# A fused transformer backward on one core: the ds tile copied as fp32 pairs, and the sums of dx through ScalarE and GpSimd

## The chip, the core and the metric

The program runs on one core of a Trainium2 chip. The metric is the device time of one execution in microseconds (us), as the median of several runs; lower is better. Engines are named as in the profile: PE (TensorE matmul), PEld (TensorE weight load), DVE (VectorE), ACT (ScalarE), POOL (GpSimd) and SP (SyncE, which issues DMAs). "L924" is line 924 of the kernel before.

## What is computed

The reference takes x (2048 tokens, 448 features), layer-normalises it, and adds to x a 16-head attention block (head size 28) and a SwiGLU block with 1792 hidden units. The kernel returns the output and, for a given gradient of it, the gradients of x and of the five weight matrices:

```python
def _fwd_reference(A_x, A_wqkv, A_wo, B_x, B_w_gate, B_w_up, B_w_down):
    x = A_x
    xn = _layernorm(x, axis=-1)
    return x + _A_ref(xn, A_wqkv, A_wo) + _B_ref(xn, B_w_gate, B_w_up, B_w_down)
...
_out, _vjp = jax.vjp(_f, A_x, A_wqkv, A_wo, B_w_gate, B_w_up, B_w_down)
```

Two pieces matter here. For each pair of heads and each block of 128 queries by 512 keys, the attention backward needs ds = exp(scores) * dp, and then the gradient of the queries, which takes ds transposed. The gradient of x is a sum over tokens of many matrix products: the gate and up paths of SwiGLU, and the gradients of q, k and v times the transposed projection weights.

## The kernel before, in words

The program is written in a fixed order per engine: what the Python code emits first on an engine runs first on it. Waits are only by data and by buffers. Up to about 617 us the forward pass and the weight gradients of SwiGLU run. What the change touches lies behind that, in the attention backward, and ends with it at about 1397 us; a tail to 1438 us finishes dx.

The attention backward is a loop over 512 steps (4 head groups, 2 head pairs, 4 key chunks, 4 query chunks, 4 query blocks of 128). Here four successive steps are called a **quad**; there are 128. On each step:

- `row` (L826) has PE compute two score tiles "sb" (L834) and, for the step before, two dp tiles "db" (L842), each 128x512 fp32 in one PSUM bank. There are three sb and three db buffers.
- `ew` (L854) has ACT take the exponential of the sb tiles into bf16 "e_sb" (L858), and DVE multiply db by e_sb into bf16 "ds_sb" (L864). Reading sb and db is what frees them.
- For the first three steps of a quad a DMA transposes ds_sb into "dsT" (L851). For the last step PE transposes it in `tr_unit` (L914): eight 128x128 bf16 transposes (L919) into one db buffer, seen there as 128x1024 bf16, and one ACT copy to dsT (L924). In the last quad alone a second one is copied by DVE (L922).
- `kv` (L926) accumulates the k and v gradients in the single PSUM tile "acc" (L937, L941). At the end of a key chunk, once in four quads, ACT copies acc out (L947, "dkv").
- `dq_unit` (L958), once per quad, multiplies dsT of the quad before into the PSUM tile "genb" (L968), and ACT copies it out: into dq_acc for the first key chunk (L972), else into dq_st (L981), which POOL then adds (L983, L985). On the last head group's last key chunk DVE does it (L977).

Between these the program places **fillers**: one unit of other work per quad, split over the four places of the step, whose products accumulate in genb, of which there is one buffer. So dq and filler units alternate in it. The unit ends behind `tr_unit` at the start of a quad, with its last matmuls and one operation that takes genb out. In order the fillers are: the last SwiGLU weight columns (`late_dw`, L898, to 662 us), y units (`y_unit`, 7 or 11 matmuls, out by DVE, L1098 and L1101, 675 to 890 us), and the units of dx that the change touches:

- `dx_unit` (L1137): 48 units, in three passes fq over the hidden units. Pass 0 has 10 matmuls a unit (L1149) and ends with an ACT copy into the fp32 SBUF sum "dxg" (L1155); it runs from 924 to 1024 us. Passes 1 (8 matmuls) and 2 (10 matmuls) end with a DVE add of genb to dxg (L1157), from 1029 to 1263 us.
- `dc_unit` (L1189): 16 units of 8 matmuls (L1196), which end with a DVE add (L1200), from 1293 to 1388 us.

Units for the q, k and v weight gradients stand between them (`dsp_unit`, `dsq_unit`, `dwq_unit`).

The order on PE around the end of a quad is: row, two filler matmuls, the eight transposes, the unit's last matmuls, row, two or three kv steps, dq, row, kv, filler matmul, row, four filler matmuls, row. On ACT the copy of L924 stands ahead of the copy of L1155, and both ahead of the next row's two exponentials.

The tail (`dx_mm`, `dx_a`, `dx_b`) reads dxg, on DVE for 13 of the 16 token blocks (L1315), and POOL adds the final terms (L1332).

Of the kernel before, what the change touches and what calls it, by code (L numbers as in the profile page):

```python
# [9 lines left out]
ALU = mybir.AluOpType  # L10
AX = mybir.AxisListType
FP32 = mybir.dt.float32
# [5 lines left out]
D = 448  # L18
# [7 lines left out]
P = 128  # L26
# [79 lines left out]
def kernel(  # L106
# [23 lines left out]
    PE, DVE, ACTE, POOL, SP = nc.tensor, nc.vector, nc.scalar, nc.gpsimd, nc.sync  # L130
# [539 lines left out]
    for t in range(4):  # L670
        run(T_unit(xnT, xn_t, t, t % 2 == 0, ps_s if t < 2 else None))
    DVE.tensor_reduce(out=r_ones[:],
                      in_=ident_f[:].rearrange("p (a b) -> p a b", b=HP)[:, :, 28:30],
# [11 lines left out]
    for c in range(3):  # L685
        k = 4 * c
        t = 4 * c + 4
# [106 lines left out]
    def have(*keys):  # L794
        for x in [x for x in slow if x[1] in keys]:
            slow.remove(x)
            SP.dma_start(out=x[2], in_=x[3])
# [23 lines left out]
    def flush(upto):  # L821
        while held and held[0][0] <= upto:
            _, o, i = held.pop(0)
            (POOL if now < NB else SP).dma_start(out=o, in_=i)
# [89 lines left out]
    def tr_unit(b):  # L914
        for qi in (3,) if b < NB // 4 - 1 else (2, 3):
            ds = dss.pop(4 * b + qi)
            ps = ps_b.tile([P, 8, P], BF16, name="db", bufs=3)
            for c in range(8):
                PE.transpose(ps[:, c, :], ds[:, c // 4, (c % 4) * P:(c % 4 + 1) * P], ident_bf[:])  # L919
            o = dsT[b][:, qi].rearrange("p j kt s -> p (j kt) s")  # L920
            if qi == 2:
                DVE.tensor_copy(out=o, in_=ps[:])  # L922
            else:
                ACTE.copy(out=o, in_=ps[:])  # L924

    def kv(k):  # L926
        g, hp, kc, qc, qi = steps[k]
# [30 lines left out]
    def dq_unit(b):  # L958
# [27 lines left out]
        if qc == 3:  # L986
            for j in range(2):
                dst = dqkvc_d[crow(g, 0, 2 * hp + j), :].rearrange("r (a q s) -> r a q s", q=2, s=P)
                for par in range(2):
                    r = 64 * par + HP * j  # L990
                    store(dst[:, :, par], dqT[g][r:r + DH, hp].rearrange("r (a s) -> r a s", s=P))
            if hp == 1:
                stream[3:3] = [(480, lambda hp=hp: dsq_unit(g, hp)) for hp in range(2)]
                at = [i for i, u in enumerate(stream) if u[1] in (dx_open, tail_open)]
                at = max(at[0] + 1, 5) if at and g != 1 else 5
                s_done.add((g, "w"))
                stream[at:at] = [(2270, lambda c=c: dwq_unit(g, c)) for c in range(4)]
# [108 lines left out]
    dxs = {}  # L1106
    dxgst = ExitStack()
# [4 lines left out]
    def dx_open():  # L1112
        flush(10 ** 9)
        yst.close()
        gp = dxgst.enter_context(tc.tile_pool(name="dxgp", bufs=1, reuse_waits="tile"))
        dxs["g"] = gp.tile([P, NT, D], FP32, name="dxg")
        st = dxst.enter_context(tc.tile_pool(name="dxp", bufs=2, reuse_waits="tile"))
        dxs["pool"] = st
        load_w(0, now + 15)
        load_dx(0, 0)  # L1120
        return
        yield

    def load_w(fq, due):
        f0, f1 = FQ[fq]
        w = dxs["w", fq] = dxs["pool"].tile([P, 5, 2, D], BF16, name="wguT")
        drip(("dx", 0, fq), [(w[:, i - f0:min(i + 2, f1) - f0], wT_d[:, i:min(i + 2, f1), :, :D]) for i in range(f0, f1, 2)], due)

    def load_dx(ch, fq):
        f0, f1 = FQ[fq]  # L1130
        if ch == 2 and fq < 2:
            load_w(fq + 1, now + 32)
        d = dxs["pool"].tile([P, 5, 2, 512], BF16, name="dau_c")
        drip(("dx", ch, fq), [(d[:, i - f0:min(i + 2, f1) - f0], F_d[ch, :, i:min(i + 2, f1), 1:3, :]) for i in range(f0, f1, 2)], now + 16)
        dxs[ch, fq] = d

    def dx_unit(ch, fq, ti):  # L1137
        if ti == 0:
            have(("dx", ch, fq))
            nxt = 4 * fq + ch + 1  # L1140
            if nxt < 12:
                load_dx(nxt % 4, nxt // 4)
        d = dxs[ch, fq]
        f0, f1 = FQ[fq]
        n = 2 * (f1 - f0)
        tsl = slice(ti * P, (ti + 1) * P)
        ps = ps_g.tile([P, 512], FP32, name="genb")
        for i in range(n):
            PE.matmul(ps[:, :D], lhsT=d[:, i // 2, i % 2, tsl], rhs=dxs["w", fq][:, i // 2, i % 2, :],  # L1149
                      start=(i == 0), stop=(i == n - 1))  # L1150
            if i < n - 1:
                yield 189
        o = dxs["g"][:, 4 * ch + ti, :]
        if fq == 0:
            ACTE.copy(out=o, in_=ps[:, :D])  # L1155
        else:
            DVE.tensor_tensor(out=o, in0=ps[:, :D], in1=o, op=ALU.add)  # L1157
        yield 189


# [23 lines left out]
    def load_dc(ch):  # L1184
        dcs[ch] = dxs["tw"].tile([P, NCP, 512], BF16, name="dc")
        src = dqkvc_d[:, ch * 512:(ch + 1) * 512].rearrange("(i p) s -> p i s", p=CP)
        drip(("dc", ch), [(dcs[ch][:CP, a:b], src[:, a:b]) for a, b in ((0, 3), (3, 6), (6, 8))], now + 16)

    def dc_unit(t):  # L1189
        if t % 4 == 0:  # L1190
            have(("dc", t // 4))
            if t < 12:
                load_dc(t // 4 + 1)
        ps = ps_g.tile([P, 512], FP32, name="genb")
        for i in range(NCP):
            PE.matmul(ps[:, :D], lhsT=dcs[t // 4][:CP, i, (t % 4) * P:(t % 4 + 1) * P], rhs=dxs["wq"][:CP, i, :],  # L1196
                      start=(i == 0), stop=(i == NCP - 1))
            if i < NCP - 1:
                yield 189
        DVE.tensor_tensor(out=dxs["g"][:, t, :], in0=ps[:, :D], in1=dxs["g"][:, t, :], op=ALU.add)  # L1200
        yield 189

    def push(*units):
# [2 lines left out]
    for ch in range(4):  # L1206
        for half in range(2):
            for ti in range(4):
                stream.append((189 * (7 + 4 * half), lambda a=(ch, half, ti): y_unit(*a)))
    stream.append((0, dx_open))  # L1210
    for fq in range(3):
        for ch in range(4):
            for ti in range(4):
                stream.append((189 * 2 * (FQ[fq][1] - FQ[fq][0]), lambda a=(ch, fq, ti): dx_unit(*a)))
    stream.append((0, tail_open))
    for t in range(NT):
        stream.append((189 * NCP, lambda t=t: dc_unit(t)))
# [119 lines left out]
    for k in range(NB + 12):  # L1337
        now = k
        if k < NB:
            g, hp, kc, qc, qi = steps[k]  # L1340
# [18 lines left out]
        if m == 0:  # L1359
            b = (k - 8) // 4  # L1360
            if 9 <= k < NB and cur is None:
                fill_open(600)
            fill_step(R0)
            if 0 <= b < NB // 4:
                tr_unit(b)
            fill_step(BIG)
        elif m == 1:
            b = (k - 13) // 4
            if 0 <= b < NB // 4:
                dq_unit(b)  # L1370
            if k > NB and k < NB + 8:
                while stream:
                    for _ in stream.pop(0)[1]():
                        pass
                if k < NB + 4:
                    dx_mm(0)
                else:
                    dx_a(0)
                    dx_mm(2)
        elif m == 2:  # L1380
            if 9 <= k < NB:
                fill_open(BIG)
                fill_step(R2)
        else:
            fill_step(R3)
# [59 lines left out]
```

## Time and profile before

| | |
|---|---|
| time, median of 3 runs | 1437.01 us |
| the three runs | 1435.54, 1437.01, 1440.87 us |
| span of the profiled execution, first to last instruction | 1438.2 us |
| attention backward, first to last exponential | about 617 to 1391 us |
| ds_sb multiplies on DVE (L864) | 1024 of 685 ns mean |
| exponentials on ACT (L858) | 1024 of 611 ns mean |
| copies of the transposed ds on ACT (L924), 128x1024 bf16 | 128 of 1016 ns mean |
| copies into dxg on ACT (L1155), 128x448 fp32 | 16 of 560 ns mean |
| adds into dxg on DVE (L1157, L1200), 128x448 fp32 | 32 of 620 ns and 16 of 616 ns mean |
| POOL adds of 128x256 fp32 (L983) and 128x512 fp32 (L396) | 724 and 1274 ns mean |

The profiled execution's own time is known as its span; it lies amid the three times and is 1.2 us above their median. A line of the timeline view holds the start, the length, the engine, the line, the operation with what it writes and reads, and how many instructions of the kind were merged; an engine starts an instruction before the one ahead has fully ended, so lengths overlap, and the distance of two starts is what an instruction takes from its engine. A line of the stage table has the stretch, its length, and then for each engine named in the header the busy time and the number of instructions, and at the end PE's granted clock, the DMA share and GB/s.

### The profile page before, as it was taken

The numbers are of one execution on the slowest core, as the hardware profiler recorded it, in microseconds if no ns is written. First come the engines' busy times: TensorE is split into PE (matmuls) and PEld (weight loads), VectorE is DVE, ScalarE is ACT, GpSimd is POOL, SyncE is SP. The second block draws the span as 40 slices with busy tenths as digits, with TensorE's granted clock in tenths as the row PEclk, the third lists the DMA queues.
The fourth block names the chain that finished last, engine by engine and source line by source line (L and its number), as shares of the span: only waits on it lengthen the run. The fifth ranks groups of instructions, "written<-read, shape, count | busy, mean of one in ns | idle before, by whom it ended". The sixth has DMA issues, their size and how long they took to land. (4 is left out here: it accounts for less than half of the span.)

```text
span 1438.2 us, 34638 instructions
## 1 busy us (share of the span) xinstructions
PE 1321.2 (92%) x12625; PEld 539.0 (37%) x12686; DVE 1154.8 (80%) x2001; ACT 1264.2 (88%) x2190; POOL 411.8 (29%) x577
## 2 busy tenths in 40 slices
PE   5899999989999999989999989999999999999995
PEld 2333333333333333333343434433443334443333
DVE  6677757656666676578999989888899999999988
ACT  4799988989889998869999989999989999899974
POOL 6574514454434454211121211201111112020005
PEclk9999999999999999989999999999999999999998
DMA  5796957796578676699999999999999999999981
GB/s 154 183 205 160 237 116 169 179 190 157 149 164 191 153 155 153 176 243 233 219 213 227 206 227 173 221 219 223 223 169 200 200 216 218 212 186 207 190 142 60
DMA packets 681116, 270.22 MB, mean 188 GB/s; under 512 B 607338, under 2 KB 655970, under 8 KB 680946
## 3 DMA queue, kind: packets, MB, share of 16 engines
q1 hardware_dynamic: 672498, 254.78, 87.1%
q0 software_dynamic: 7040, 12.93, 4.1%
q8 instruction: 99, 1.62, 0.5%
q14 instruction: 71, 0.58, 0.1%
q10 hardware_dynamic: 1408, 0.30, 0.1%
HBM read 64.37 MB, written 59.62 MB: 86 GB/s over the span
## 5 line engine op out<-in xcount | busy, mean ns | idle before, releaser
L864 DVE TENSOR_TENSOR ds_sb<-db,e_sb 128x512 bf16<-128x512 f32 x1024 | 646.5, 685 | 48.6 <-issue 22.4
L858 ACT ACTIVATE e_sb<-sb 128x512 bf16<-128x512 f32 x1024 | 555.0, 611 | 53.7 <-PE db L842 37.1
L628 ACT ACTIVATE eT<-s_w 128x1024 bf16<-128x1024 f32 x256 | 263.8, 1030 | 47.0 <-PE s_ps L625 43.8
L630 ACT ACTIVATE eT<-s_ps 128x512 bf16<-128x512 f32 x512 | 280.2, 611 | 0.0
L842 PE MATMUL db<-kd,qd 32*128 32x512 bf16 x1024 | 238.0, 385 | 8.6 <-DVE ds_sb L864 7.5
L834 PE MATMUL sb<-kd,qd 32*128 32x512 bf16 x1024 | 210.9, 389 | 5.3 <-DMA qd<-QD_d 3.4
L983 POOL TENSOR_TENSOR dq_acc<-dq_acc,dq_st 128x256 f32<-128x256 f32 x64 | 46.4, 724 | 497.7 <-ACT dq_st L981 497.7
L941 PE MATMUL acc<-ds_sb,qd 128*32 128x512 bf16 x1024 | 161.3, 391 | 0.0
L937 PE MATMUL acc<-e_sb,qd 128*32 128x512 bf16 x1024 | 159.2, 392 | 1.3 <-DVE dw_o L544 1.3
L924 ACT COPY dsT<-db 128x1024 bf16<-128x1024 bf16 x128 | 130.0, 1016 | 18.4 <-PE db L919 17.3
L396 POOL TENSOR_TENSOR nn<-nn,ag 128x512 f32<-128x512 f32 x56 | 71.3, 1274 | 249.7 <-DVE ag L394 241.1
L625 PE MATMUL s_ps<-QQ,KK 32*128 32x512 bf16 x512 | 126.2, 385 | 4.1
L1149 PE MATMUL genb<-wguT,dau_c 128*128 128x448 bf16 x448 | 117.5, 355 | 6.3 <-ACT dq_st L981 3.9
L625 PE MATMUL s_w<-QQ,KK 32*128 32x512 bf16 x512 | 100.2, 387 | 12.8 <-ACT eT L628 9.8
L834 PEld LDWEIGHTS <-qd 32*128 32x128 bf16 x1024 | 48.2, 91 | 146.3 <-issue 136.9
L437 PE MATMUL gen<-xn_t,f_sp 128*128 128x448 bf16 x416 | 91.8, 354 | 2.6 <-DVE nn L411 1.7
L437 PEld LDWEIGHTS <-f_sp 128*128 128x128 bf16 x640 | 55.7, 98 | 76.7 <-issue 31.6
L919 PE MATMUL db<-ident_bf,ds_sb 128*128 128x128 bf16 x1032 | 80.3, 222 | 0.9 <-DVE ds_sb L864 0.9
L968 PE MATMUL genb<-dsT,kd 128*32 128x256 bf16 x2048 | 79.2, 274 | 1.1
L919 PEld LDWEIGHTS <-ds_sb 128*128 128x128 bf16 x1032 | 69.1, 99 | 23.6 <-issue 5.1
L397 POOL TENSOR_TENSOR nn<-nn,tt 128x512 f32<-128x512 f32 x56 | 72.1, 1287 | 4.4
L625 PEld LDWEIGHTS <-KK 32*128 32x128 bf16 x1024 | 29.1, 91 | 115.3 <-issue 112.5
(179 smaller groups left out, 1951.7 us busy)
## 6 DMA issues: line engine op xcount, KB each, us to landing
F_d<-hda SPq DMA_DIRECT2D x56, 384.0 KB
dau_c<-F_d SPq DMA_DIRECT2D x24, 512.0 KB
qd<-QD_d SPq DMA_DIRECT2D x16, 512.0 KB
kd<-KD_d SPq DMA_DIRECT2D x16, 384.0 KB
dsT<-ds_sb SPq DMA_TRANSPOSE x383
h_c<-F_d SPq DMA_DIRECT2D x8, 512.0 KB
wT_d<-wT_f SPq DMA_DIRECT2D x14, 256.0 KB
KD_d<-qk_sp SPq DMA_DIRECT2D x7, 512.0 KB
```

The costliest lines, as they stand in the source:

```text
L437: PE.matmul(ps[:, :D], lhsT=fsp[fc][:, t // 4, w, t % 4, :], rhs=rhs[:, t, :], start=(t == 0), stop=(t == NT - 1))
L625: PE.matmul(sp4[hh], lhsT=KK[g][r:r + HP, kt * P:(kt + 1) * P], rhs=QQ[g][r:r + HP, qsl], start=True, stop=True, tile_position=(r, 0))
L628: ACTE.activation(out=e2[0][:], in_=wide[:], func=ACT.Exp, scale=SCALE)
L630: ACTE.activation(out=e2[1][:, j], in_=sp4[2 + j], func=ACT.Exp, scale=SCALE)
L834: PE.matmul(s_ps[:], lhsT=qside[g, qc][r:r + HP, 0, qi * P:(qi + 1) * P], rhs=kside[g, kc][r:r + HP, 0, :], start=True, stop=True, tile_po ...
L842: PE.matmul(d_ps[:], lhsT=qside[g, qc][r:r + HP, 1, qi * P:(qi + 1) * P], rhs=kside[g, kc][r:r + HP, 1, :], start=True, stop=True, tile_po ...
L858: ACTE.activation(out=est[k][:, j], in_=sps.pop((k, j))[:], func=ACT.Exp, scale=SCALE)
L864: DVE.tensor_tensor(out=ds[:, j], in0=dps.pop((k - 1, j))[:], in1=est[k - 1][:, j], op=ALU.mult)
L919: PE.transpose(ps[:, c, :], ds[:, c // 4, (c % 4) * P:(c % 4 + 1) * P], ident_bf[:])
L924: ACTE.copy(out=o, in_=ps[:])
L937: PE.matmul(a[r:r + HP, :], lhsT=sp4[:, 1, r:r + HP], rhs=e[:, j, :], start=first, stop=last, tile_position=(0, r), skip_group_check=True)
L941: PE.matmul(a[r:r + HP, :], lhsT=sp4[:, 0, r:r + HP], rhs=ds[:, j, :], start=first, stop=last, tile_position=(0, r), skip_group_check=True)
```

## The change

The copy of the transposed ds by ACT reads and writes its 128x1024 bf16 as 128x512 fp32, the same bytes. The copy by DVE for the last quad stays. The 48 adds into dxg leave DVE: ACT copies genb to an fp32 staging tile "gst" (two buffers), and POOL adds that to dxg. Pass 0 still copies directly. No instruction of PE or SP is added or moved.

```diff
             if qi == 2:
                 DVE.tensor_copy(out=o, in_=ps[:])
             else:
-                ACTE.copy(out=o, in_=ps[:])
+                ACTE.copy(out=o.bitcast(FP32), in_=ps[:].bitcast(FP32))
...
         dxs["g"] = gp.tile([P, NT, D], FP32, name="dxg")
+        dxs["st"] = dxgst.enter_context(tc.tile_pool(name="gsp", bufs=2, reuse_waits="tile"))
...
+    def add_in(o, ps, first):
+        if first:
+            ACTE.copy(out=o, in_=ps[:, :D])
+            return
+        st = dxs["st"].tile([P, D], FP32, name="gst")
+        ACTE.copy(out=st[:], in_=ps[:, :D])
+        POOL.tensor_tensor(out=o, in0=o, in1=st[:], op=ALU.add)
...
-        o = dxs["g"][:, 4 * ch + ti, :]
-        if fq == 0:
-            ACTE.copy(out=o, in_=ps[:, :D])
-        else:
-            DVE.tensor_tensor(out=o, in0=ps[:, :D], in1=o, op=ALU.add)
+        add_in(dxs["g"][:, 4 * ch + ti, :], ps, fq == 0)
...
-        DVE.tensor_tensor(out=dxs["g"][:, t, :], in0=ps[:, :D], in1=dxs["g"][:, t, :], op=ALU.add)
+        add_in(dxs["g"][:, t, :], ps, False)
```

## The prediction

> **What bounds the kernel now.** I read the page's busy shares first, then the table of stages over the attention backward, then the timelines of single quads.
>
> ```profile
> PE 1321.2 (92%) x12625; PEld 539.0 (37%) x12686; DVE 1154.8 (80%) x2001; ACT 1264.2 (88%) x2190; POOL 411.8 (29%) x577
> ```
>
> Three engines look nearly full, so the shares decide nothing. By stages (busy us of PE, PEld, DVE, ACT, POOL):
>
> ```profile
> core 0: us, PE busy (x) PEld busy (x) DVE busy (x) ACT busy (x) POOL busy (x), PEclk, DMA share, GB/s
> 924.10:1009.50 85.40, 81.68 (x926) 33.63 (x925) 70.87 (x113) 81.54 (x159) 9.80 (x14) 1.00 1.13 222
> 1029.00:1160.40 131.40, 126.07 (x1461) 52.75 (x1458) 123.27 (x214) 121.72 (x227) 17.91 (x28) 1.00 1.06 196
> 1160.40:1262.50 102.10, 97.66 (x1135) 41.92 (x1134) 96.04 (x156) 93.62 (x175) 13.97 (x21) 0.98 1.15 214
> ```
>
> The first row is pass 0, where ACT copies into dxg: ACT is busy 95%, DVE 83%. The others are passes 1 and 2, where DVE adds: DVE 94%, ACT 93 and 92%. So pass 0 is ACT's, and in the others it is open whether DVE's add is on the path. The timelines tell. Pass 0, ACT and then PE:
>
> ```profile
> 948.53 1.02 ACT L924 COPY dsT<-db 128x1024 bf16<-128x1024 bf16 x1
> 949.42 0.56 ACT L1155 COPY dxg<-genb 128x448 f32<-128x448 f32 x1
> 949.85 1.13 ACT L858 ACTIVATE e_sb<-sb 128x512 bf16<-128x512 f32 x2
> ...
> 954.44 1.02 ACT L924 COPY dsT<-db 128x1024 bf16<-128x1024 bf16 x1
> 955.33 0.56 ACT L1155 COPY dxg<-genb 128x448 f32<-128x448 f32 x1
> ```
> ```profile
> 954.21 0.73 PE L1149 MATMUL genb<-wguT,dau_c 128*128 128x448 bf16 x3
> ...
> 955.46 0.38 PE L937 MATMUL acc<-e_sb,qd 128*32 128x512 bf16 x2
> ...
> 955.94 0.62 PE L968 MATMUL genb<-dsT,kd 128*32 128x256 bf16 x16
> ```
>
> A quad takes 954.44-948.53 = 5.91 us. The unit's product is complete at 954.94 (954.21+0.73), but ACT is in L924 and takes genb out only from 955.33 to 955.89. The dq products (L968) need genb and start at 955.94. PE's last kv pair starts 955.46 and occupies 0.22 (kv pairs follow each other at 0.22), so PE stood idle about 0.25.
>
> Pass 1, DVE and then PE:
>
> ```profile
> 1125.66 0.62 DVE L1157 TENSOR_TENSOR dxg<-genb,dxg 128x448 f32<-128x448 f32 x1
> 1126.19 1.28 DVE L864 TENSOR_TENSOR ds_sb<-db,e_sb 128x512 bf16<-128x512 f32 x2
> 1127.63 3.74 DVE L864 TENSOR_TENSOR ds_sb<-db,e_sb 128x512 bf16<-128x512 f32 x6 [0.16 <-ACT dq_acc L972]
> 1131.29 0.62 DVE L1157 TENSOR_TENSOR dxg<-genb,dxg 128x448 f32<-128x448 f32 x1
> ```
> ```profile
> 1130.26 0.61 PE L919 MATMUL db<-ident_bf,ds_sb 128*128 128x128 bf16 x8
> ...
> 1130.99 0.39 PE L834 MATMUL sb<-kd,qd 32*128 32x512 bf16 x2
> 1131.00 0.80 PE L842 MATMUL db<-kd,qd 32*128 32x512 bf16 x2
> 1131.72 0.39 PE L937 MATMUL acc<-e_sb,qd 128*32 128x512 bf16 x2
> ```
>
> The quad takes 1131.29-1125.66 = 5.63. The two db products of the row at 1131.00 took 0.80 where a pair takes 0.39: the second waits for its buffer, which the last of the six multiplies frees at 1131.37 (1127.63+3.74). So the ring is: six multiplies on DVE, second db, kv and dq on PE, next row, its db, first of the next six multiplies. **The add lies outside it.** DVE does the add and two multiplies while PE goes through kv and dq, and DVE is idle before the next six (the 0.16 above), waiting for the row. A quad with 7-matmul y units has the same 5.63 (timeline, L924 at 747.50 and 753.13), and the quad from 675.05 to 680.74, with no DVE add in it, took 5.69. Pass 2, with two more matmuls, takes 5.69 (L924 at 1171.79 and 1177.48); y units with 11 take 5.85 (L924 at 771.07 and 776.92): there PE sets the pace.
>
> Once in four quads ACT copies acc out as well (L947, 0.72). There ACT is the path: pass 1 takes 6.31 (L924 at 1130.93 and 1137.24), pass 0 6.75 (935.87 and 942.62).
>
> **The change, part by part.** The built program has the same PE and SP orders; ACT gains 48 copies, DVE loses 48 adds, POOL gains 48 adds.
>
> *The pair copy.* No row shows it. Bounds: 1.016 us if it goes by bytes, as now; 0.56 (L1155, 448 fp32 to fp32) as the nearest smaller row. Per element: L924's 1024 in 1.016 and L858's 512 in 0.61 differ by 0.8 ns an element, L858 and L1155 by 0.8 as well, though L1155 moves 1792 bytes a partition in 0.56 and L924 2048 in 1.016. So elements count, and I take 0.61. Start to start L924 takes 0.89, an exponential 0.49: 0.40 less for ACT, 128 times, 51 us of ACT's 1264. It pays only where ACT is the path:
>
> - Pass 0, 12 plain quads: the copy to dxg starts when the product is complete, 954.99 instead of 955.33, and dq no longer waits: 0.25 each, 3.0 us. Next late is the ring above and PE, as in pass 2 (5.69), which 5.91-0.25 = 5.66 meets.
> - Pass 0, 4 quads with the acc copy: ACT is the path through copy, exponentials, L947 and dq's copy, and all start 0.33 earlier (again bound by the product): 1.3 us.
> - Quads with the acc copy in the y units and late_dw, where ACT is the path (645, 692, 741, 788, 862): L947 moves up until acc is complete. At 741: acc complete at 742.81, L947 now at 743.05, new 742.87: 0.18 each, 0.9 us.
> - Elsewhere nothing: L924 is done long before dsT is read a quad later, and its db buffer is wanted only by the second row behind it (1127.08, free at 1126.32).
>
> *The db buffers.* The built program hands the three db buffers out in another order in the first quads. In quads 1, 6, 7, 8 (633, 663, 669, 675) the row behind the transposes has the transposes' own buffer for its second db, so it waits for ACT's copy instead of DVE. At 669: copy 669.16+0.61 plus 0.06 is 669.83, now 669.71: 0.12 later, three times; at 633 about 0.4. A loss of 0.8 us. From quad 9 the order is as before.
>
> *ACT for DVE in passes 1 and 2 and dc.* DVE loses 48 x 0.54 (start to start at 1125.66) = 26 us. In plain quads of pass 1 and dc the ring does not hold it: 0. In pass 2 the two multiplies behind the add start 0.10 sooner, which spares PE a short wait for ds: 0.04 each, 12 quads, 0.5 us. With L977 on DVE and at the last unit some 0.3 us. ACT: pair copy 0.49 and new copy 0.43 are 0.92 where L924 took 0.89: 0.03 later exponentials, hidden in plain quads by ACT's own wait (0.20 before the L858 at 1129.96). Cover gone, they cost that 0.03 a quad, 1.4 us. In the 13 quads with the acc copy ACT is the path: 9 at 0.05, and 4 of pass 2, where the product is complete 0.1 later, at 0.12: a loss of 0.9 us. Behind the new copy on ACT stand the exponentials, and dq on PE waits for genb: 1125.79 to 1126.35, wanted at 1126.54.
>
> *POOL.* A 448 add lies between 0.724 (256) and 1.274 (512): about 1.14 by the line through both. A unit comes each 5.7 us and POOL is busy 0.7 of them; staging has two buffers: hidden, and dxg is read first at 1397.54, the last add ending near 1389.5. Beside DVE: in the tail L1318, with both inputs in SBUF, goes from 0.63 to 1.58 beside POOL's L1332. L864 has one input in PSUM: its six took 3.74 beside a POOL add (from 1150.83) and 3.74 without (from 1127.63). I take 0; at the tail's price, 0.95 for each of 48, it would be 46 us.
>
> [...]
>
> **Sum.** -3.0-1.3-0.9+0.8-0.5-0.3+0.9 = **-4.3 us**. The profiled 1438.2 becomes 1433.9; against the median of the runs, 1.2 below that span, 1437.0-4.3 = **1432.7**.
>
> **Rivals.**
>
> - *The db wait goes with the adds.* If the rows of passes 1, 2 and dc stop waiting for db, a quad falls near PE's own pace: 5.41, as from L924 at 1114.27 to 1119.68, where no row waited over 0.20 for db. 23 plain quads x 0.21 and 12 x 0.15 more: 6.6 us, so about **1426**. For: DVE is at 94% there. Against: the add is outside the ring.
> - *ACT becomes the path, slower.* If the pair copy goes by bytes (0.89 start to start), all 48 units pay what pass 0 pays: 35 x 0.25 and 13 x 0.44 = 14.5 us, and pass 0 gains nothing: **1452**. It decides from 0.62 start to start, where genb comes free later than dq wants it. Against: L1155's row.
> - *POOL slows DVE*, at most as above. Against: the two 3.74.
> - *Not doing what it says* is excluded for the work by the built program; the gains could drown in the granted clock (0.94 from 633 to 690): 1437.
>
> **How the numbers follow.** Forecast 0.60, db wait gone 0.22, ACT or POOL the path 0.08, drowned 0.10. A measurement of this kernel can tell about 0.5%, 7.2 us, from no change: faster is under 1429.8, slower over 1444.2. Faster takes the first rival and a little of the forecast, 0.28; slower the second and a little more, 0.10; same 0.62. The range reaches from the first rival to the drowned case and the loss of cover (1437+1.4): 1425 to 1439; the 0.08 above and some edges are left out.
>
> **What would show it.** Right: L924 at about 0.61; pass 0 quads at 5.65 and 6.4; pass 1 and dc still 5.63 with the db pair at 0.80 behind the transposes; POOL adds near 1.14; L864 at 685 ns. Wrong: pass 1 quads near 5.4 (first rival) or 5.9 with dq waiting for genb (second); L864 longer beside POOL.

## The result, and the profile after

| | before | after |
|---|---|---|
| time, median of 15 runs each, taken in turn | 1440.31 us | 1433.52 us |
| range of the runs | 1435.54 to 1443.47 | 1429.76 to 1439.40 |
| span of the profiled execution | 1438.2 us | 1428.8 us |
| PE's granted clock in the profiled execution | 0.982 | 0.982 |

The ratio is 0.9967, with a 95% interval of 0.9952 to 0.9982: a gain of 4.8 us by the ratio. The forecast was 4.3 us, with 0.62 for a change that stays under 0.5%. The median itself lies 0.8 us from the forecast 1432.7, and that is in part luck: the kernel before, 1437.01 in the three runs that the forecast started from, has 1440.31 in the fifteen, and the two medians differ by 6.8.

Page, after: the busy shares.

```profile
PE 1319.6 (92%) x12625; PEld 541.5 (38%) x12686; DVE 1130.3 (79%) x1953; ACT 1234.7 (86%) x2238; POOL 465.1 (33%) x625
```

ACT lost 29.5 us of work and DVE 24.5; POOL gained 53.3. The time fell by a tenth of what ACT and DVE lost together: the work that left was beside the path almost everywhere. The groups of after say what the changed operations cost (after the bar: busy us, mean ns of one, then the idle time of the engine before them):

```profile
L864 DVE TENSOR_TENSOR ds_sb<-db,e_sb 128x512 bf16<-128x512 f32 x1024 | 646.0, 684 | 68.2 <-ACT dsT L924 22.0 <-issue 12.5 <-ACT e_sb L858 9.2
L924 ACT COPY dsT<-db 128x512 f32<-128x512 f32 x128 | 75.5, 590 | 17.2 <-PE db L919 14.3 <-PE genb L1021 1.9
L1131 POOL TENSOR_TENSOR dxg<-dxg,gst 128x448 f32<-128x448 f32 x48 | 54.6, 1138 | 194.0 <-ACT gst L1130 194.0
```

The pair copy takes 590 ns where the bf16 copy took 1016. The POOL add takes 1138. DVE's multiplies did not grow beside it (684, before 685).

The stages of after, with the same quads in the rows as the three rows of the prediction (us; then busy us of PE, PEld, DVE, ACT, POOL; granted clock, DMA share, GB/s):

```profile
921.80:1003.10 81.30, 79.59 (x926) 34.26 (x925) 70.97 (x113) 76.88 (x159) 9.78 (x14) 1.00 1.15 221
1021.60:1153.00 131.40, 126.02 (x1458) 53.29 (x1458) 115.79 (x197) 119.51 (x244) 35.47 (x43) 1.00 1.10 206
1153.00:1253.20 100.20, 96.40 (x1136) 42.00 (x1135) 88.18 (x141) 93.15 (x191) 30.97 (x36) 1.00 1.09 214
```

Pass 0 went from 85.40 to 81.30. Pass 1 stayed at 131.4 (from its first L924 to the first of pass 2 131.22 before, 131.40 after), although DVE does 7.5 us less and ACT 2.2 us less in it. Pass 2 went from 102.10 to 100.20, but that is no gain of the change: three quads of it, 95, 96 and 100 (counted from 1 at the first L924), took 20.86 and now take 18.85. The first two hold a stretch of half PE clock in before (1206.6 to 1210.0); the third took 7.41, and in it DVE waited 0.88 for the DMA that transposes ds (its multiplies start again at 1235.30), which it does not do after. The rest of pass 2 is even in sum.

Compared quad by quad (from one L924 to the next), by kinds, with the quads that hold a stretch of half clock in either profile left out:

| quads | before | after | each | sum over those seen |
|---|---|---|---|---|
| pass 0, plain (11) | 5.91 | 5.63 | -0.28 | -3.04 |
| pass 0, with the acc copy (3) | 6.75 | 6.36 | -0.38 to -0.39 | -1.15 |
| late_dw and y, with the acc copy (5) | 6.31, one 6.34 | 6.18 | -0.13 to -0.16 | -0.69 |
| behind a dsp or dsq unit (5) | 5.42, one 5.52 | 5.30, one 5.41 | -0.11 to -0.12 | -0.60 |
| pass 2, plain (10) | 5.66, 5.69, two 5.83 | 5.63, 5.82, 5.74 | -0.03 to -0.06, two -0.01 and -0.09 | -0.45 |
| pass 1 and dc, plain (14) | 5.63 | 5.63 | 0.00 | 0.03 |
| pass 1 and dc, with the acc copy (7) | 6.31, one 6.88 | 6.32, one 6.89 | +0.01 | 0.07 |
| quad 87 and pass 2, with the acc copy (4) | 6.30 | 6.37 to 6.53 | +0.06 to +0.22 | 0.53 |

These sum to -5.3 us, and that is not the whole loop. The twelve quads with half clock took 3.0 more after, and the quads without it that are in no row 3.2 less; three of those, 34, 35 and 100, took 3.26 less, since DVE in before waited in them 0.58, 1.66 and 0.88 for the DMA that transposes ds. Such waits come and go: quads 33 to 38 take from 35.3 to 38.6 us in the ten profiles that have no half clock there. So it is chance that the two cancel, and the loop as a whole is 5.5 us shorter. The 9.4 us between the two spans hold 4.1 us more that lie ahead of the first L924 (633.25 against 629.17), where nothing was changed: in the eleven profiles of this study the loop begins anywhere from 629.2 to 634.5 us.

### The profile page after: what moved, and what is told of

It reads as the page before. It is cut to its first block, busy times and chain, and to the rows that moved or that the text cites. A ratio compares the mean times of both kernels' runs of the same rounds, so it can differ in the third digit from the quotient of the medians.

```text
span 1428.8 us, 34695 instructions
## 1 busy us (share of the span) xinstructions
PE 1319.6 (92%) x12625; PEld 541.5 (38%) x12686; DVE 1130.3 (79%) x1953; ACT 1234.7 (86%) x2238; POOL 465.1 (33%) x625
## 5 line engine op out<-in xcount | busy, mean ns | idle before, releaser
L864 DVE TENSOR_TENSOR ds_sb<-db,e_sb 128x512 bf16<-128x512 f32 x1024 | 646.0, 684 | 68.2 <-ACT dsT L924 22.0
L842 PE MATMUL db<-kd,qd 32*128 32x512 bf16 x1024 | 240.9, 385 | 6.8 <-DVE ds_sb L864 4.1
L1131 POOL TENSOR_TENSOR dxg<-dxg,gst 128x448 f32<-128x448 f32 x48 | 54.6, 1138 | 194.0 <-ACT gst L1130 194.0
L924 ACT COPY dsT<-db 128x512 f32<-128x512 f32 x128 | 75.5, 590 | 17.2 <-PE db L919 14.3
```

Of the source, the lines that this page charges most:

```text
L842: PE.matmul(d_ps[:], lhsT=qside[g, qc][r:r + HP, 1, qi * P:(qi + 1) * P], rhs=kside[g, kc][r:r + HP, 1, :], start=True, stop=True, tile_po ...
L864: DVE.tensor_tensor(out=ds[:, j], in0=dps.pop((k - 1, j))[:], in1=est[k - 1][:, j], op=ALU.mult)
```

## The experiments

**1. The pair copy alone.**

```diff
-                ACTE.copy(out=o, in_=ps[:])
+                ACTE.copy(out=o.bitcast(FP32), in_=ps[:].bitcast(FP32))
```

> The kernel before with the pair copy alone; the adds into dxg stay on DVE. Theory (the pair copy is the gain, and DVE's adds lie off the path): the 16 pass 0 quads gain what the changed kernel showed, 13 x 0.28 and 3 x 0.38, 4.8 us; the quads with the acc copy gain 0.13 each, in the y units (5) and, since ACT gets no new copy, also in passes 1, 2 and dc (13): 2.3 us; the first quads lose about 0.8. Together -6.3 us, ratio 0.9956, a little under the changed kernel's 0.9967; pass 1 quads stay 5.63, pass 2 quads 5.69. Rival (part of the gain comes from DVE's relief): ratio above 0.9975, and some quads of passes 1, 2 or dc longer than in the changed kernel by more than 0.06.

Measured: 1434.76 us (12 runs), ratio 0.9956, interval 0.9938 to 0.9974. Pass 0 and the quads behind dsp units are as in the full change. Pass 2's plain quads stay at 5.66 and 5.69, and the acc quads of pass 1 and dc go from 6.31 to 6.17, where the full change has 6.32. So the pair copy alone carries the gain. Moving the adds on top of it saves 0.03 to 0.06 a plain quad in pass 2 and costs 0.15 in each of those acc quads and 0.10 to 0.17 in those of pass 2 (6.27 here); the two kernels can't be told apart by their times.

**2. The adds alone** (L924 as before).

```diff
...
-        o = dxs["g"][:, 4 * ch + ti, :]
-        if fq == 0:
-            ACTE.copy(out=o, in_=ps[:, :D])
-        else:
-            DVE.tensor_tensor(out=o, in0=ps[:, :D], in1=o, op=ALU.add)
+        add_in(dxs["g"][:, 4 * ch + ti, :], ps, fq == 0)
...
```

> The kernel before with the adds through ACT and POOL alone; the transposed tile is copied as bf16. Theory: every unit of passes 1, 2 and dc then pays what pass 0 pays in the kernel before, with L924 at 1.016 us: plain quads 5.63 to 5.91, quads with the acc copy 6.31 to 6.75, 35 x 0.27 + 13 x 0.44 = 15 us, ratio 1.0105, dq waiting for genb. Rival (DVE's adds are on the path, their leaving pays for the copy on ACT): ratio 1.003 or less.

Measured: 1455.44 us, ratio 1.0104, interval 1.0075 to 1.0133. Pass 1 quads go from 5.63 to 5.91, pass 2 from 5.69 to 5.91, acc quads from 6.31 to 6.75. The timelines of ACT and then PE in one quad of pass 1 (start, length, engine, line):

```profile
1142.75 1.02 ACT L924 COPY dsT<-db 128x1024 bf16<-128x1024 bf16 x1
1143.64 0.56 ACT L1130 COPY gst<-genb 128x448 f32<-128x448 f32 x1
```
```profile
1142.52 0.35 PE L1158 MATMUL genb<-wguT,dau_c 128*128 128x448 bf16 x1
...
1143.77 0.38 PE L937 MATMUL acc<-e_sb,qd 128*32 128x512 bf16 x2
1144.25 0.62 PE L968 MATMUL genb<-dsT,kd 128*32 128x256 bf16 x16
```

The unit's product is complete at 1142.87, but genb is free only at 1144.20, since ACT is in L924 until 1143.64. PE's last kv pair gives way at 1143.99, and dq starts at 1144.25: 0.26 of idle PE a quad, what pass 0 paid before. The quads are what was expected, to the hundredth. It is the price that the second rival of the prediction named (14.5 us; the medians differ by 14.1), and it is what the move of the adds costs without the shorter copy.

**3. The db buffers in the old order** (the change as it is, with one db buffer after the other).

```diff
+    def db_tile(shape, dtype):
+        turn[0] += 1
+        return ps_b.tile(shape, dtype, name=f"db{turn[0] % 3}", bufs=1)
...
```

> The changed kernel with the three db buffers handed out strictly in turn, which is the order of the kernel before in all quads but the last. Theory: only quads 1, 6, 7, 8 change; they were reckoned to lose 0.8 us, so the ratio is 0.9961 against 0.9967. Rival (the whole loss of 3.9 us that the changed kernel's profile shows in its first eight quads is the buffers'): ratio 0.994, the first eight quads as in the kernel before. If PE's granted clock made that loss, the quads with 0.6 us matmuls lie elsewhere or show in this run too.

Measured: 1438.61 us (12 runs), ratio 0.9984, interval 0.9965 to 1.0003; the change's own was 0.9952 to 0.9982. No gain. In the trace of after the four waits are where the prediction put them; the list of waits, 621 to 1391 us (waiting instruction, releaser: us in total, times, longest), and one of them on PE:

```profile
PE db L842 <- ACT dsT L924: 1.2, 4, 0.3
```
```profile
661.21 0.37 PE L842 MATMUL db<-kd,qd 32*128 32x512 bf16 x1 [0.31 <-ACT dsT L924]
```

Quad 6 takes 5.65 with this wait and 5.56 without it: 0.09. But the order acts further on too, where the prediction took it to be as before: quads 9 and 12 to 14 together take 0.27 less in after than here, most of it in quad 12 (5.63 against 5.96; 5.96 in before too). Why stays open. And quads 1, 7 and 8 stay long with the old order too (7.16, 7.27, 8.38; in after 8.41, 7.14, 7.23). What makes them long is PE's clock. The stage table of after (the last column but two is the granted clock):

```profile
629.20:637.60 8.40, 7.68 (x56) 2.78 (x53) 5.27 (x9) 4.73 (x10) 0.00 (x0) 0.59 1.09 238
660.60:681.00 20.40, 18.42 (x178) 6.50 (x176) 15.41 (x26) 16.16 (x32) 2.17 (x3) 0.83 1.11 232
```

In before the same quads had 0.73 and 0.91, with the old order in this experiment 0.62 and 0.75. In the eleven profiles quads 7 and 8 take at most 6.02 without a stretch of half clock (5.89 and 5.69 in before) and at least 7.04 with one (7.14 and 7.23 in after). So in the quads where the clock lets one see it the new order costs 0.09 in one and gains more in others, and it is not what made the time of this run.

**4. Is the wait for db the path in a plain quad?** The kernel before, with one db buffer after the other as in experiment 3, and the row behind the transposes split: its second db product is issued behind the kv steps.

```diff
-                row(k)
-                ew(k)
+                if m == 1:
+                    row(k, js=(0,))
+                    ew(k, ds_=False)
...
+        if m == 1 and K0 <= k <= NB:
+            row(k, js=(1,), sb=False)
+            ew(k, ex=False)
```

> The kernel before, db buffers in turn; in the row behind the transposes PE does the kv steps ahead of the second db, which waits there for DVE's last multiply. Theory (the ring: six multiplies, second db, kv and dq, next row): the wait of 0.42 is filled with two kv steps of 0.22, so plain quads of 5.63 fall to about 5.4, some 75 quads x 0.2 = 15 us, ratio near 0.989, and the next limit is ACT or PE. Rival (5.63 is PE's own pace or DVE's total): within 0.3% of the kernel before, DVE or PE waiting elsewhere for what was gained.

Measured: 1453.76 us, ratio 1.0113, interval 1.0075 to 1.0151: slower, where the ring theory asked for faster. Quads with 7 filler matmuls went from 5.63 to 5.47, with 8 from 5.63 to 5.65, with 10 (pass 2) from 5.69 to 6.02, with 11 from 5.85 to 6.21. The row on PE in pass 2:

```profile
1174.73 0.39 PE L840 MATMUL sb<-kd,qd 32*128 32x512 bf16 x2
1174.74 0.38 PE L848 MATMUL db<-kd,qd 32*128 32x512 bf16 x1
1175.05 0.39 PE L943 MATMUL acc<-e_sb,qd 128*32 128x512 bf16 x2
...
1175.60 0.39 PE L848 MATMUL db<-kd,qd 32*128 32x512 bf16 x1
1175.91 0.62 PE L974 MATMUL genb<-dsT,kd 128*32 128x256 bf16 x16
```

The three products left in the row start within 0.01 of each other and take 0.32 from PE (1174.73 to 1175.05), as long as the four of the next row do (1176.47 to 1176.79). The one taken out takes 0.31 by itself (1175.60 to 1175.91). So the experiment removed a wait and added at least 0.31 of PE work to each quad. Without that wait the quad now grows with its matmuls: 5.47, 5.65, 6.02, 6.21 for 7, 8, 10 and 11, 0.18 to 0.19 each, which is what one filler matmul takes from PE (four in a line take 0.93, one 0.36). So here PE sets the pace. Less the 0.31 of added work, PE could do a quad with 7 or 8 matmuls in at most 5.16 or 5.34 (an estimate). So such a quad is not at PE's pace before or after the change: it has 5.63 for both, as the ring asks. After the change a quad with 10 matmuls has 5.63 too, and PE still waits in it: its rows at 945.53 and 948.05 take 0.36 and 0.42 from PE, where a row takes 0.32. So the ring is the likelier limit there as well; no run tests that by itself.

**5. The kv steps ahead of the whole row** (the kernel before with one db buffer after the other, and two kv steps ahead of the row behind the transposes; the four products stay together).

```diff
+            if m == 1:
+                while kv_n < NB and kv_n <= k - 3 and not (kv_n % 16 == 15):
+                    kv(kv_n)
+                    kv_n += 1
             if k >= K0:
                 row(k)
```

> The kernel before, db buffers in turn; two kv steps stand ahead of the whole row behind the transposes, so that its four products stay together (taking the second db out of them had cost PE 0.33 a quad). Theory (ring through DVE): the row finds its buffers free, and the next limit is DVE's own round, the row's 0.53 to the first multiply and eight multiplies of 0.61, 5.4 to 5.5 where the quads of 7 and 8 matmuls take 5.63; pass 0 (ACT's) stays 5.91. Rival (the next row then waits for the same multiplies, the wait only moves): 5.60 to 5.65.

Measured: one run, 1469.4 us, span 1467.6. Quads with 7 matmuls go from 5.63 to between 5.55 and 5.58, those with 8 from 5.63 to between 5.74 and 5.77, those of pass 0 from 5.91 to 6.15, those with 11 by about 0.46 to 6.33. The wait has moved. ACT and then PE in quad 87, with the acc copy:

```profile
1172.53 1.09 ACT L864 ACTIVATE e_sb<-sb 128x512 bf16<-128x512 f32 x2
...
1174.07 0.40 ACT L987 ACTIVATE dq_st<-genb 128x256 f32<-128x256 f32 x1
```
```profile
1174.52 0.35 PE L1155 MATMUL genb<-wguT,dau_c 128*128 128x448 bf16 x1 [0.74 <-ACT dq_st L987]
```

The row came at 1172.11, behind two kv steps, and its exponentials start at 1172.53. ACT takes dq out of genb at 1174.07 to 1174.47, and the filler on PE waits 0.74 for that, where it waits 0.52 in the same quad of before. In a plain quad of pass 2 (from 1184.03) ACT is idle for 0.42 until the late row comes, and the row behind that one takes 0.72 from PE (1185.91 to 1186.63) where a row takes 0.32. So the wait only moves, as the rival had it; but the rival's 5.60 to 5.65 was met by neither kind of quad.

**6. Is ACT the path in the acc quads?** The change, with the copy of acc (L947) on DVE, which now has room.

```diff
-            ACTE.activation(out=dkv[g, hp][:, kc * 512:(kc + 1) * 512], in_=a[:], func=ACT.Copy,
-                            scale=(sc_a if hp == 0 else sc_b)[:, 0:1])
+            DVE.tensor_scalar(out=dkv[g, hp][:, kc * 512:(kc + 1) * 512], in0=a[:],
+                              scalar1=(sc_a if hp == 0 else sc_b)[:, 0:1], scalar2=None, op0=ALU.mult)
```

> The changed kernel with the copy of acc (once in four quads, 0.72 on ACT) on DVE, as a multiply by the same column. Theory (in these quads ACT is the path, and DVE has the room that the adds left): the 31 such quads fall from 6.2 to 6.5 to about 5.75, 0.55 each, 17 us, ratio to the kernel before near 0.985. Rival (these quads are long because of their third kv step on PE, or DVE's ring grows by the copy's 0.6): ratio 0.994 or more.

Measured: 1438.81 us (12 runs), ratio 0.9987, interval 0.9970 to 1.0003: no gain. Acc quads of pass 1 and dc go from 6.32 to 6.18, but those of y from 6.18 to 6.37 (one to 6.72) and 6.46 to 6.77, of pass 0 from 6.36 to 6.47, of pass 2 from between 6.37 and 6.44 to 6.47. DVE and PE in one of pass 1:

```profile
1130.67 0.74 DVE L947 TENSOR_SCALAR dkv<-acc,cols 128x512 bf16<-128x512 f32 x1
1131.40 1.89 DVE L864 TENSOR_TENSOR ds_sb<-db,e_sb 128x512 bf16<-128x512 f32 x3
```
```profile
1130.86 0.39 PE L842 MATMUL db<-kd,qd 32*128 32x512 bf16 x2
...
1131.69 0.61 PE L834 MATMUL sb<-kd,qd 32*128 32x512 bf16 x2
1131.93 0.59 PE L842 MATMUL db<-kd,qd 32*128 32x512 bf16 x2
```

The db tiles of 1130.86 are complete at 1131.25, but DVE is in the copy until 1131.40. The next row's second sb waits for an exponential (to 1131.87), its second db for DVE, 0.2 each. So ACT was the path in these quads, but DVE's ring stands close behind it, and the copy now lengthens the ring: the 0.57 that ACT is spared (after, L947 at 1125.10 to the next start at 1125.67) comes out as 0.14 gained in pass 1 and mostly 0.03 to 0.3 lost elsewhere.

**7. The same with the adds on DVE** (pair copy, adds as before, acc copy on DVE).

> The pair copy alone, adds left on DVE, and the copy of acc on DVE too. Theory: between two groups of six multiplies DVE has about 2.2 us; the add 0.54, two multiplies 1.22 and the copy 0.6 are 2.36, so these quads of passes 1, 2 and dc take about 5.9 instead of 5.75 in the run with the adds on ACT and POOL: ratio near 0.986, 0.001 to 0.002 worse than that run. Rival (DVE has room anyway, ACT is better off without the new copy): the same or better than that run.

Measured: 1440.82 us, ratio 1.0013, interval 0.9991 to 1.0036. The gain expected was not there, as in experiment 6, probably for the same reason; with the adds on DVE as well, the acc quads of pass 1 take 6.37 (6.18 with the pair copy alone) and those of pass 2 6.59 (6.27).

**8. Both rearrangements together** (the change, acc copy on DVE, kv steps ahead of the whole row as in experiment 5).

> The changed kernel with both: acc copied by DVE, kv steps ahead of the row behind the transposes, db buffers in turn. Theory: the gains add, 0.985 less 36 to 70 plain quads of 0.1 to 0.16 (4 to 11 us), ratio 0.978 to 0.982. Rival (the wait only moves): ratio as with the acc copy alone.

Measured: 1478.32 us, ratio 1.0280, interval 1.0248 to 1.0312. Pass 0 and pass 2 plain quads 6.14, those with the acc copy 6.66 to 7.04. Nothing of the expected gain came: the later row holds ACT's exponentials also when ACT has less to do. In a plain quad of pass 2 (from 1188.31) ACT is idle for 0.33 ahead of them.

**9. Each add where it fits.** In the quads with the acc copy DVE takes the unit out, in the others ACT and POOL as in the change.

```diff
     def add_in(o, ps, first):
+        if now % 16 == 0:
+            if first:
+                DVE.tensor_copy(out=o, in_=ps[:, :D])
+            else:
+                DVE.tensor_tensor(out=o, in0=ps[:, :D], in1=o, op=ALU.add)
+            return
```

> The change as it is, except that DVE takes the unit's product out in the quads in which ACT also copies acc out: four units of pass 0 by a DVE copy, thirteen later ones by the old DVE add. ACT is the path in those quads, and in the others the add beside the multiplies is what costs. The theory that only these quads distinguish the two ways expects: pass 0 quads with the acc copy from 6.36 to about 6.18, those of pass 1 and dc from 6.32 to 6.17 (as the kernel with the pair copy alone has them), those of pass 2 from 6.37-6.44 to about 6.25, all plain quads as after the change (5.63, pass 2 too). Sum against the change: 3 x 0.18 + 8 x 0.15 + 3 x 0.15 + 0.35 for the quad from 1144.8 = 2.5 us, so a ratio to the kernel before of about 0.995 where the change has 0.9967. A rival: a DVE instruction of 0.62 between units by ACT and POOL makes DVE wait for POOL's last add of the sum or makes the multiplies late, and the quads stay at 6.32 or above: 0.9967 or more.

Measured: 1435.00 us (12 runs), ratio 0.9971, interval 0.9950 to 0.9991. In the trace the quads did what was asked: pass 0 with the acc copy 6.36 to 6.24 (expected 6.18), pass 1 and dc 6.32 to 6.18, pass 2 6.37-6.44 to 6.24, quad 87 (from 1146.47 in after; the expectation's "quad from 1144.8") 6.53 to 6.18, plain quads of pass 2 at 5.63. One dc quad, 115, went from 6.32 to 6.53. In the acc quads without half clock this is 2.2 us better than the change, but 0.35 of it is quad 87, which has 6.31 in experiment 3 with the change's adds, and over all quads without half clock it is 1.2 us. The time does not show it: 0.9971, where the change has 0.9967.

**How far the times can tell these apart.** Each run lists PE's mean granted clock. Over the 63 runs of the kernel before that were taken beside experiments 1 to 9 the clock went from 0.973 to 0.985 and the time from 1448.31 to 1432.88, and a line through them, 1440.2 us at 0.980 and 1.01 us less for each 0.001, leaves a scatter of 2.1 us; the clock holds two thirds of the variance. An estimate at equal clock is the mean distance of a kernel's runs from this line (the interval is that of the mean alone). The line's own place is uncertain by as much: the runs of the kernel before that were taken beside experiments 1 to 4 lie 0.4 us above it, those beside 5 to 8 0.2 above, those beside 9 0.8 below. The clocks of the 15 that were taken beside the change are not on record, so its -6.3 is not against its own neighbours, as the 4.8 us of the ratio are.

| kernel | runs | against before at equal clock, us (95%) |
|---|---|---|
| the change | 15 | -6.3 +- 1.1 |
| pair copy alone | 12 | -6.6 +- 1.5 |
| old db order | 12 | -4.1 +- 1.2 |
| each add where it fits | 12 | -5.0 +- 1.4 |
| change, acc copy on DVE | 12 | -3.7 +- 1.4 |
| pair copy, acc copy on DVE | 12 | -0.7 +- 1.2 |
| adds alone | 4 | +15.8 +- 3.1 |

The traces say that row four should not be behind row one, and row three by a few tenths at most (experiment 3). So about 2 us remain that neither the clock nor the kinds of quads explain. Waits for the DMA that transposes ds are a candidate: quads 33 to 38 take 37.8 us in before, with 2.2 of such waits, and 35.3 in after, with none. But one profile a kernel can't show it. The four best kernels can't be ranked by time here. No version that beats the change was shown.

## Why the prediction was right, point by point

- **The pair copy goes by elements: right.** Taken 0.61, measured 0.590. With the same bytes in half the elements the copy takes 426 ns less (1016 - 590): 0.83 ns for each of the 512 elements less, where the prediction had 0.8 from two pairs of rows of before.
- **Pass 0 gains 0.25 in a plain quad and 0.33 in an acc quad: right in mechanism, a little small.** Measured 0.28 and 0.39. The prediction let the gain end at pass 2's 5.66 to 5.69 and called that PE's pace. It was not: with the adds off DVE pass 2 falls to 5.63 with the same matmuls on PE, and with the pair copy alone it does not (experiment 1). The timeline of after, ACT and then PE:

```profile
945.64 0.53 ACT L1127 COPY dxg<-genb 128x448 f32<-128x448 f32 x1
```
```profile
944.87 0.73 PE L1158 MATMUL genb<-wguT,dau_c 128*128 128x448 bf16 x3
...
946.12 0.38 PE L937 MATMUL acc<-e_sb,qd 128*32 128x512 bf16 x2
946.33 0.61 PE L968 MATMUL genb<-dsT,kd 128*32 128x256 bf16 x16
...
948.05 0.49 PE L842 MATMUL db<-kd,qd 32*128 32x512 bf16 x2
```

  The product is complete at 945.60, the copy takes it 0.04 later, and dq starts 0.21 behind the kv pair at 946.12, which is that pair's own time: ahead of dq no idle PE is left. What is left is a wait for db: the pair at 948.05 took 0.49 where a pair takes 0.39, as in pass 1.
- **The acc quads of late_dw and y gain 0.18: right in place, 0.13 to 0.16 measured.**
- **"Elsewhere nothing": wrong, by about 1 us.** Quads behind a dsp or dsq unit went from 5.42 to 5.30 (one from 5.52 to 5.41), five times in quads without half clock in both traces, and also with the pair copy alone; three more show 5.29 or 5.30 in the profiles of the other kernels that have the pair copy: 1.0 us in all. The prediction used one of them, from 1114.27 to 1119.68, as an example of PE's own pace. It was not. ACT and PE in it before, then both in the same quad after:

```profile
1115.18 1.09 ACT L858 ACTIVATE e_sb<-sb 128x512 bf16<-128x512 f32 x2
```
```profile
1115.72 0.49 PE L834 MATMUL sb<-kd,qd 32*128 32x512 bf16 x2
```
```profile
1107.17 1.09 ACT L858 ACTIVATE e_sb<-sb 128x512 bf16<-128x512 f32 x2
```
```profile
1108.13 0.39 PE L834 MATMUL sb<-kd,qd 32*128 32x512 bf16 x2
```

  The first exponential of 1115.18 ends near 1115.78 and frees the sb buffer that the second product of the row at 1115.72 wants; the pair took 0.49 where a pair takes 0.39, and the kv step behind it came 0.44 after the row's start. Counted from L924 (1114.27 before, 1106.69 after) these exponentials start 0.91 behind it before and 0.48 after, the row's pair takes 0.39, and the kv step comes 0.33 after the row's start: 0.11 of the 0.12.
- **The ring: right.** Pass 1 and dc did not move (5.63), with DVE in pass 1 down from 94% to 88% (115.79 of 131.40 us). The db pair behind the transposes is still stretched in after:

```profile
1129.63 0.81 PE L842 MATMUL db<-kd,qd 32*128 32x512 bf16 x2
```

  Experiment 4 shows that 5.63 is not PE's pace there. It does not show that the ring can be cut at a gain: all three tries paid more than they freed. The first rival, which let the wait go with the adds, is out.
- **Pass 2 plain 0.04: right, 0.03 to 0.06.**
- **The acc quads under the moved adds lose 0.05, in pass 2 0.12: half right.** The seven of pass 1 and dc lost 0.01 against before, since the copy to gst takes back the 0.14 that the pair copy alone gains there (experiment 1). Pass 2 lost 0.06 to 0.14 (0.10 to 0.17 against the pair copy alone). The 0.22 of quad 87 is not the change's: experiment 3, with the same adds, has 6.31 there. The sum measured is 0.6 with that quad and 0.4 without it, where 0.9 was taken.
- **The db buffers: the waits right, the loss not shown.** The waits are there, in four quads, 1.2 us of PE waiting in all; 0.09 of the 0.31 in quad 6 reached the end, where 0.12 was taken. The 0.4 of quad 1 could not be seen beside the clock. And quads 9 and 12 to 14, where the prediction had nothing, are 0.27 shorter in the new order, so not even the sign of the 0.8 is shown.
- **POOL hidden: right.** The add takes 1138 ns, and L864 takes 684 with it in the loop (685 before). Why L1318 grows beside L1332 in the tail (0.63 to 1.58 us in before) and L864 does not grow beside the add was not shown.
- **The sum.** The rows of the table give -5.3 where the terms gave -4.3, and several misses lie behind the 1.0 between them. The 0.8 of the db buffers has no row. The quads behind dsp units, 0.6, were missed, and the moved adds cost 0.3 less. The other way, 0.3 taken for L977 and the last unit has no row, and the rows of pass 0 (14 of 16 quads), of y and of pass 2 hold 0.4 less than their terms. So the sum is closer than its parts, and that is luck too.

## What to carry to other kernels

ACT's copy of 16-bit data out of PSUM became little more than half as long (590 ns for 1016) by calling the data fp32 pairs, but it paid only in the stages where ACT is the path: 54 us less on ACT (128 times 0.426) were worth about 6. Taking work from a 94% busy engine changed nothing in pass 1 (quads of 5.63 before and after), since the work lies outside the loop of waits that sets the pace; find such a loop by comparing stages with different amounts of work and the same period. Before a product is moved out of a wait, look whether it runs together with others, and what it costs alone.

## What the runs showed of the hardware

- Up to the end of the loop PE's granted clock falls to half (0.50) in stretches of 3.4, 6.8 or 10.2 us by the records of before and after, six of ten in before and seven of nine in after in the first 70 us and from 610 to 690 us, where the loop begins. Later ones are few, and their places are not random: the five between 690 and 1380 us (before, from 721.95, 1015.50 and 1206.64; after, from 721.74 and 817.31) all lie in the last but one of sixteen quads (quads 15, 31, 63 and 95). PE was busy for only 2.12 to 2.31 of the 3.41 us ahead of each. Not every such pause is followed by one (before, 1109.80 to 1113.21: 2.12 of 3.41 us, and the clock stays at 1.00), and which of them are differs from run to run; what decides it was not shown. A pair of matmuls that takes 0.39 takes 0.61 in such a stretch (after, 667.16, "acc", two 128x512). The mean clock goes with two thirds of the variance of the times of one kernel, 1.01 us for 0.001, and that kernel's runs spread over 15 us, more than any difference between the better versions here.
- Four products over 32 rows each (sb and db, `32*128` in the lines) that are issued together cost PE 0.32 us, three also 0.32, and a single one, issued apart, 0.31 (experiment 4).
- A multiply on DVE can wait for the DMA that transposes ds, by 0.58, 1.66 and 0.88 us in quads 34, 35 and 100 of before, and not at all in the same quads of after.
